# Moving loads and token products between units of a fused RWKV-6 and SiLU-MLP kernel

## The chip, the core and the metric

The kernel runs on one core of a Trainium2 chip. The metric is device time in microseconds, from the start of the program to its end, as a median of several runs. Besides TensorE (PE, with its weight loads PEld), the core has VectorE (DVE), ScalarE (ACT) and GpSimd (POOL); SyncE (SP) issues nearly all DMAs of this kernel, one behind the other.

## The reference

Inputs r, k, v, w have the shape (4 batches, 8 heads, 768 steps, 48). The first part is a recurrence over time, for every batch and head:

```python
state = zeros(48, 48)
for t in range(768):
    y[t] = r[t] @ (state + outer(u * k[t], v[t]))
    state = w[t][:, None] * state + outer(k[t], v[t])
```

The second part takes y as x, 3072 tokens of 384 numbers: `h = x @ w_in` (384 to 2048), `g = h * sigmoid(h)`, `out = g @ w_out` (2048 to 384). Everything is float32.

## The kernel before, in words

**Units.** Time is cut into six blocks of 128 steps and the batches into two pairs: 12 units of 256 tokens (two batches), numbered 0 to 11. Within a unit the recurrence is rewritten as a triangular matrix of scores. Level l of 0 to 6 holds the pairs of steps that lie in neighbouring blocks of 2^l steps; queries (`tr`), keys (`tk`) and products of decays (`tw`) grow from level to level. The diagonal, and in later units all of the small blocks, are not made by matmuls but by products and sums of r, k, u and w in token order: the bonus (`NTOK` is 2, `NPAIR` 4, `NSLOT` 2, `FIRST` 3).

- `level` and `burst` (L698, L706) are the score matmuls, with `keep_level` and `keep_masked` (L716) copying them through a mask into `score`. `prepare` (L774, L621 in `grow_queries`) makes the queries of the next levels on VectorE, and `grow_keys` (L639, L648) the keys on GpSimd.
- Units 0 to 3 form their diagonal with `bonus` (GpSimd, L442 to L446) and `bonus_sum` (VectorE, L451 and L455), which in units 2 and 3 ends with four DMAs into `diag` (L461); `bonus_spread` (L589 to L592) and `bonus_write` (L598) put it into the scores. From unit 4 on `block_bonus` (L501), `block_sum` (L535), `block_move` (L554 to `kept` in memory, L557 back), `block_spread` (L562 to L565) and `block_write` (L571) do this for blocks of eight steps. `load_rk` brings what these need in token order (L107 in units up to 3, L153 later).
- `load_blocks` (L123) brings w, r and k of a unit for the transposes of `turn` (L374), 16 DMAs for each of the three; `raw` has two slots, so a unit's loads may begin when the unit two before it has been turned.
- `y_state`, `y_values` (L847, L855) and `update` (L882) make y and the new state; `move_x` (L918) carries y over ten DMAs to `xt`, the input of the second part.

**Second part.** `up` (L990, then SiLU on ACT at L999) and `down` (L1012) are its two products. From unit 1 on `quarter` (L1056 and the additions L1065) does the second product by a Strassen-like scheme of seven products of 128x192 tiles per half; its operands are sums of halves of g (`sums`, L1038) and four differences of quarters of w_out (`weight_sums`, L1030), each made once.

**Weights.** In the first 100 us the weights of the second part are fetched in 16 pieces (L206) and rounded piece by piece: ACT (L223, L231), VectorE (L242, L243 in `join_weight`) and GpSimd (L255 in `add_weight`).

**Order.** Everything is issued in an order written out by hand: for units 0 to 2 as long `do(...)` lists, after that by `mix(i)`, which returns groups of steps of unit i, with which ups of unit i − 1 and quarters of unit i − 2 are interleaved. Each engine runs its own instructions in that order. Loads of `raw` for coming units are spread over the groups by

```python
loads = block_loads(i + NSLOT) if i + NSLOT < len(units) else []
```

so in `mix(i)` the w, k and r of unit i + 2 are asked for.

Of the kernel before, what the change touches and what calls it, by code (L numbers as in the profile page):

```python
# [8 lines left out]
F32 = mybir.dt.float32  # L9
# [29 lines left out]
def kernel(  # L39
# [11 lines left out]
    nc = tc.nc  # L51

    B, H, S, D = r.shape
    DM, DF = moe_w_in.shape
    L = 128
    NL = 7
    NB = 2
    NP = H // 2
# [7 lines left out]
    units = [(n, b0) for n in range(S // L) for b0 in range(0, B, NB)]  # L66
    NSLOT = 2
    NTOK = 2
    NPAIR = 4
    FIRST = 3  # L70
# [5 lines left out]
    pt = ctx.enter_context(tc.tile_pool(name="pt", bufs=2))  # L76
# [102 lines left out]
    tokens_rk = const.tile([128, 2, H, 2, D], F32, name="tokens_rk")  # L179
# [4 lines left out]
    spare = const.tile([128, NSPARE * 2 * TU], F32, name="spare")  # L184

    def rk(i, x):
        if i < NTOK:
            return twos(raw[:, i % NSLOT, 1 + x])[0].rearrange("p h (s d) -> p h s d", s=2)
        return tokens_rk[:, x]
# [143 lines left out]
    NSC = 1  # L333
    score = const.tile([128, NSC, 2, Q, L], F32, name="score")

    masks = {}
    first = {}
    for l in range(NL):
        c, ni = 1 << l, L >> (l + 1)
# [89 lines left out]
    ruk = {}  # L429
# [4 lines left out]
    def bonus(i, x):  # L434


        engine = nc.gpsimd if i > 0 or x == 0 else nc.vector
        if x == 0:
            ruk[i] = tokens_rk[:, 1] if i < NTOK else pt.tile([128, H, 2, D], F32, name="ruk", bufs=1)

            ruk[i, 0] = tokens_rk[:, 0, :, 0] if i < NTOK else ruk[i][:, :, 0]
            engine.tensor_tensor(out=ruk[i, 0], in0=rk(i, 0)[:, :, 1], in1=rk(i, 1)[:, :, 0], op=ALU.mult)  # L442
        elif x == 1:
            engine.tensor_tensor(out=ruk[i], in0=rk(i, 0), in1=rk(i, 1), op=ALU.mult)
        else:
            engine.tensor_tensor(out=ruk[i], in0=ruk[i], in1=u_bc[:, :, None, :].to_broadcast([128, H, 2, D]), op=ALU.mult)  # L446
# [18 lines left out]
    at = 768  # L465
# [207 lines left out]
    def dims_of(have, start, *dims):  # L673
        return bass.AP(tensor=have.tensor, offset=have.offset + start, ap=[have.ap[0], *dims])

    def corner(l, x):

        return x % 2, x if x % 2 == 0 else (L >> l) - 1 - x
# [2 lines left out]

    def score_products(i, l, queries, sc):
        c, ni = 1 << l, L >> (l + 1)
        if i > 0 or l == NL - 1:
            for p in range(NP):
                for x in range(4 if c == 32 else 2):
                    for e in range(2):
                        rows = slice(PD * e, PD * e + D)
                        if c >= 32:
                            b, first = corner(l, x)  # L690
                            q = (p, 2 * NP - 1 - p)[b]
                            to, have = sc[e][x * c:(x + 1) * c, q, first // 2 * c:(first // 2 + 1) * c], queries[rows, q, (first + 1) * c:(first + 2) * c]
                        else:
                            apart = 2 * (NP - p) - 1
                            to = dims_of(sc[e][x * 64:(x + 1) * 64, p, :], 32 * x, [apart * L // 2 + 32 - 64 * x, 2], [1, 32])
                            have = dims_of(queries[rows, p, :], 64 * x + c, [apart * L + 64 - 128 * x, 2], [2 * c, 32 // c], [1, c])
                        m = 32 if c == 32 else 64
                        nc.tensor.matmul(to, lhsT=tk[i][rows, X[l % 2] + p, x * m:(x + 1) * m], rhs=have, start=True, stop=True)  # L698
            return

        for p in range(NP):
            for e in range(2):
                rows = slice(PD * e, PD * e + D)

                apart, r_p, s_p = 2 * (NP - p) - 1, queries[rows, p, :], sc[e][:, p, :]
                nc.tensor.matmul(bass.AP(tensor=s_p.tensor, offset=s_p.offset,  # L706
                                         ap=[s_p.ap[0], [apart * L // 2, 2], [1, L // 2]]),
                                 lhsT=tk[i][rows, X[l % 2] + p, :],
                                 rhs=bass.AP(tensor=r_p.tensor, offset=r_p.offset + c,
                                             ap=[r_p.ap[0], [apart * L, 2], [2 * c, ni], [1, c]]),  # L710
                                 start=True, stop=True)
# [66 lines left out]
    made = {}  # L778
# [8 lines left out]
    def keep_level(i, l):  # L787
        c = 1 << l
        for e in range(2):
            if c < 32 and (i > NTOK or l == FIRST):  # L790
                keep_masked(i, l, e, made[i, l])
                continue
            for x in range(4 if c == 32 else 2):
                if c >= 32:
                    b, first = corner(l, x)
                    nc.scalar.copy(
                        out=score[x * c:(x + 1) * c, i % NSC, e, b * NP:(b + 1) * NP, (first + 1) * c:(first + 2) * c],
                        in_=made[i, l][e][x * c:(x + 1) * c, b * NP:(b + 1) * NP, first // 2 * c:(first // 2 + 1) * c])
                    continue
                rows = slice(x * 64, (x + 1) * 64)  # L800
                for b in range(NB):
                    half, inner = (x, 1 - x)[b], [1, c]
                    nc.vector.copy_predicated(
                        out=dims_of(score[rows, i % NSC, e, b * NP, :], 64 * half + c, [L, NP], [2 * c, 32 // c], inner),
                        mask=dims_of(masks[l][rows, b], 32 * half, [0, NP], [c, 32 // c], inner),
                        data=dims_of(made[i, l][e][rows, b * NP, :], 32 * half, [L // 2, NP], [c, 32 // c], inner))

    def go_on(i, l):

# [112 lines left out]
    def both(fn, i, *args):  # L922
        return [(fn, i, b, *args) for b in range(NB)]

    def block_loads(i):
        return [(load_blocks, i, name, g) for name in "wkr" for g in range(4)]

    def mix(i):

        ahead = i + 1 < len(units)  # L930
# [37 lines left out]
                      [(block_spread, i), (block_write, i)],  # L968
                      [(burst, i, 5), (keep_level, i, 5), (keep_level, i, 6), (go_on, i, 6)], *end]

        loads = block_loads(i + NSLOT) if i + NSLOT < len(units) else []
        if i + 1 < len(units):
            loads.insert(len(loads) // 2, (load_values, i + 1))

        behind = groups[10 if i < NPAIR else 1:]
        for at, group in enumerate(behind):
            group += loads[at * len(loads) // len(behind):(at + 1) * len(loads) // len(behind)]
        return groups
# [61 lines left out]
    ob, partial = {}, {}  # L1040
# [42 lines left out]
    def do(*steps):  # L1083
        for fn, *args in steps:
            fn(*args)
# [16 lines left out]
    blocks = block_loads(2)  # L1102
# [3 lines left out]
    for l in range(1, NL):  # L1106
# [8 lines left out]
       (up, 0, 2))  # L1115


    others = {1: blocks[8:12], 2: [(bonus_sum, 1, 0), (bonus_sum, 1, 1), (load_rk, 2), *both(update, 0)],
              3: [(bonus_spread, 1), (reverse_v, 1), (clear, 1), (load_values, 2)]}

    def piece(i):
# [3 lines left out]
    for m in range(1, 4):  # L1125
# [1 line left out]
    do((head_weight, 8), (join_weight, 7), (scores, 1, 5), (grow_keys, 1, 6), (add_weight,), (tail_weight, 8), (up, 0, 6),  # L1127
       (bonus_write, 1))

    do((scores, 1, NL - 1), (join_weight, 8), (add_weight,), (up, 0, 7), *both(y, 1), (turn_apart, 1),  # L1130
       (tail_weight, 9), (turn_k, 1), (dense_x, 1, 0), (head_weight, 9, [0]), (dense_x, 1, 1), (head_weight, 9, [1]),
       (join_weight, 9), (add_weight,), (tail_weight, 10), (head_weight, 10), *both(update, 1), (up, 1, 0), *both(turn, 2, "w"))
    blocks = block_loads(3)

    others = {0: [(up, 1, 1), (down, 0, 0, 0), *both(turn, 2, "k"), (product, 2, 0), (product, 2, 1)],
# [4 lines left out]
    for m in range(6):  # L1140
# [2 lines left out]
    second.append(ctx.enter_context(tc.tile_pool(name="po", bufs=1, space=bass.MemoryType.PSUM)))  # L1143

    blocks = block_loads(4)
    do(*blocks[0:2], (level, 2, 2), (prepare, 2, 3), (weight_sums, 1), (down, 0, 1, 0), (down, 0, 0, 3), (down, 0, 1, 1),
       (sums, 1, 0), (bonus, 2, 0), (bonus_sum, 2, 0))
    do(blocks[2], (burst, 2, 3), (keep_level, 2, 3), (keep_level, 2, 4), (go_on, 2, 4), (prepare, 2, 5), (bonus, 2, 1),
       (bonus, 2, 2), (down, 0, 1, 2), (bonus_sum, 2, 1), (load_rk, 3), (sums, 1, 1), *blocks[3:7], (down, 0, 1, 3))
    do((burst, 2, 5), (keep_level, 2, 5), (keep_level, 2, 6), (go_on, 2, 6), (up, 1, 6), (bonus_spread, 2), (bonus_write, 2),  # L1150
       (load_values, 3), (turn_apart, 2), (turn_k, 2), (up, 1, 7), (sums, 1, 2))
    do((sums, 1, 3), (y_state, 2), *both(y_values, 2), *both(update, 2),
       (move_x, 2),
       *blocks[7:])
# [1 line left out]
    for i in range(3, len(units)):  # L1156
        steps = downs(i - 2) + ups(i - 1)
        groups = mix(i)
        if i == NTOK + 1:

            groups[2].append((weight_sums, 2))
            groups[4].insert(1, (weight_sums, 3))
        room = (1, 1, 0, 2, 1, 1, 1, 1, 1, 2, 2, 1, 1, 0) if i < NPAIR else (3, 2, 2, 1, 1, 1, 2, 1, 1, 1, 0)
        for group, count in zip(groups, room):
            do(*group)
            for step in steps[:count]:
                do(*step)
            steps = steps[count:]
# [32 lines left out]
```

## Time and profile before

| what | before |
| --- | --- |
| median of 3 runs | 612.0 us (609.66 to 613.12) |
| profiled execution, its time | 611.3 us |
| its span | 609.5 us |
| mean granted TensorE clock | 0.997 of full speed |
| TensorE busy | 594.1 us, 97% |
| TensorE weight loads | 530.7 us, 87% |
| VectorE | 423.8 us, 70% |
| GpSimd | 367.2 us, 60% |
| ScalarE | 232.7 us, 38% |

All durations are from one profiled execution. A group's line of the timeline gives its start, how long it ran, the engine, the line of the kernel, the operation, output and inputs, the size, and in brackets the idle time of that engine before it with the instruction that ended it. Each float32 matmul of the program stands as two in the counts (L990: 576 calls, x1152). A line of SyncE is the issue of a DMA, not its transfer.

### The profile page before, as it was taken

What the parts mean: (1) busy time and instruction counts of PE and PEld (TensorE: products, weight loads), DVE (VectorE), ACT (ScalarE), POOL (GpSimd) and SP (SyncE); (2) the same over time, 40 slices, a digit from 0 to 9 for tenths busy, and PEclk for the clock granted to TensorE, in tenths of its full rate; (3) what the DMA queues carried; (4) which work ended last, traced back from release to release, by engine and by line L of the source; (5) the groups of instructions that cost most, each with busy time, mean ns of one, the idle gap of its engine ahead of it and who ended that gap; (6) DMA issues with size and microseconds to landing.
All of it is one profiled execution on the core that took longest, in us unless ns stands there. A gap on an engine that the chain in (4) does not pass through costs nothing.

```text
span 609.5 us, 15190 instructions
## 1 busy us (share of the span) xinstructions
PE 594.1 (97%) x5998; PEld 530.7 (87%) x5998; DVE 423.8 (70%) x715; ACT 232.7 (38%) x516; POOL 367.2 (60%) x414
## 2 busy tenths in 40 slices
PE   8999999899999997999999999999999999999997
PEld 7778876699889897889889889989989989989997
DVE  7879779898795495587588587487587597561041
ACT  6799792431530440351351252242252242241110
POOL 6998488557667278378468578568568658500000
PEclk9999999999999998999999999999999999999999
DMA  9966774353543643643543552552452312100000
GB/s 222 300 164 169 147 232 49 72 98 48 128 62 53 135 61 53 129 65 52 121 70 53 113 80 51 108 89 50 97 95 48 81 44 53 36 3 27 26 1 26
DMA packets 203079, 53.44 MB, mean 88 GB/s; under 512 B 186752, under 2 KB 194816, under 8 KB 203008
## 3 DMA queue, kind: packets, MB, share of 16 engines
q1 hardware_dynamic: 201424, 51.88, 41.6%
q8 instruction: 47, 0.77, 0.6%
q10 hardware_dynamic: 1584, 0.59, 0.4%
q14 instruction: 24, 0.20, 0.1%
HBM read 43.21 MB, written 5.24 MB: 79 GB/s over the span
## 4 chain that ended last, share of the span: by engine, by line
PE 72%; DVE 12%; DMA 4%; POOL 3%; ACT 3%; issue 3%; SPq 3%; DVEq 0%; POOLq 0%; ACTq 0%
PE p_h L990 31%; PE p_o L1056 30%; PE p_m L855 2%; DVE score L716 2%; DVE temps L1038 2%; DVE tr L621 2%; SPq L123 2%; PE p_sc L698 2%; POOL tk L639 2%; PE p_m L698 1%; DMA raw<-in_w_dram 1%; PE p_m L847 1%; DMA tokens_w<-in_w_dram 1%; DVE p_w L242 1%; DMA raw<-in_r_dram 1%
## 5 line engine op out<-in xcount | busy, mean ns | idle before, releaser
L990 PE MATMUL p_h<-xt,w_in_sb 128*128 128x256 f32 x1152 | 258.9, 382 | 1.8 <-POOL w_in_sb L255 1.1
L990 PEld LDWEIGHTS p_h<-xt,w_in_sb 128*128 128x128 f32 x1152 | 215.9, 190 | 32.8 <-POOL w_in_sb L255 1.2
L999 ACT ACTIVATE gt<-p_h 128x512 f32<-128x512 f32 x90 | 53.3, 596 | 189.2 <-PE p_h L990 188.8
L639 POOL TENSOR_TENSOR tk<-tk,tw 128x256 f32<-128x256 f32 x128 | 93.7, 753 | 43.5 <-issue 22.9
L1056 PE MATMUL p_o<-own,temps 128*128 128x192 f32 x528 | 90.2, 331 | 4.5 <-DVE temps L1065 4.5
L1056 PEld LDWEIGHTS p_o<-own,temps 128*128 128x128 f32 x528 | 87.6, 193 | 5.4 <-DVE temps L1065 5.3
L1056 PE MATMUL p_o<-w_out_sb,gt 128*128 128x192 f32 x508 | 87.4, 328 | 0.0
L1056 PEld LDWEIGHTS p_o<-w_out_sb,gt 128*128 128x128 f32 x508 | 82.7, 190 | 0.9 <-issue 0.4
L501 POOL TENSOR_TENSOR ruk<-tokens_rk 128x768 f32<-128x768 f32 (+1 forms) x32 | 50.0, 1573 | 52.0 <-DMA tokens_rk<-in_k_dram 31.9
L1038 DVE TENSOR_TENSOR temps<-gt 128x256 f32<-128x256 f32 x84 | 56.9, 677 | 22.4 <-ACT gt L999 22.4
L621 DVE TENSOR_TENSOR tr<-tr,tw 128x512 f32<-128x512 f32 x61 | 56.4, 924 | 15.3 <-PE p_m L698 12.4
L422 POOL TENSOR_TENSOR tw<-tw 128x256 f32<-128x256 f32 (+6 forms) x83 | 43.3, 521 | 36.4 <-DVE tw L374 32.5
L609 ACT COPY tk<-tk 128x256 f32<-128x256 f32 x52 | 20.9, 403 | 99.0 <-POOL tk L639 71.7
L1065 DVE TENSOR_TENSOR partial<-p_o,partial 128x192 f32<-128x192 f32 x33 | 11.8, 358 | 38.9 <-PE p_o L1056 38.7
L1038 DVE TENSOR_TENSOR temps<-temps,gt 128x256 f32<-128x256 f32 x43 | 32.1, 748 | 1.5
L716 DVE COPY_PREDICATED score<-mask,p_sc 128x512 f32<-128x512 int8 x42 | 31.1, 795 | 2.7 <-PE p_sc L698 2.5
L1056 PE MATMUL p_o<-w_out_sb,temps 128*128 128x192 f32 x176 | 30.4, 326 | 0.0
L1065 DVE TENSOR_TENSOR temps<-p_o,partial 128x192 f32<-128x192 f32 x22 | 7.9, 357 | 31.9 <-PE p_o L1056 22.4
L860 ACT COPY yt<-p_m 48x512 f32<-48x512 f32 x40 | 23.2, 581 | 14.9 <-PE p_m L855 8.7
L1056 PEld LDWEIGHTS p_o<-w_out_sb,temps 128*128 128x128 f32 x176 | 28.9, 190 | 0.0
L698 PEld LDWEIGHTS p_sc<-tr,tk 48*32 48x32 f32 (+1 forms) x1312 | 18.1, 119 | 11.6 <-issue 6.3
L501 POOL TENSOR_TENSOR spare<-tokens_rk 128x384 f32<-128x384 f32 (+1 forms) x16 | 28.1, 1754 | 0.0
(180 smaller groups left out, 845.7 us busy)
## 6 DMA issues: line engine op xcount, KB each, us to landing
w_out_sb<-in_moe_w_in_dram SPq DMA_DIRECT2D x6, 768.0 KB, 7.5
w_out_sb<-in_moe_w_out_dram SPq DMA_DIRECT2D x4, 768.0 KB, 5.2
own<-in_moe_w_out_dram SPq DMA_DIRECT2D x4, 768.0 KB, 5.9
tokens_rk<-in_r_dram SPq DMA_DIRECT2D x8, 384.0 KB, 4.4
tokens_rk<-in_k_dram SPq DMA_DIRECT2D x8, 384.0 KB, 5.3
tokens_w<-in_w_dram SPq DMA_DIRECT2D x8, 384.0 KB, 6.5
xt<-yt SPq DMA_DIRECT2D x60, 48.0 KB, 2.0
raw<-in_w_dram SPq DMA_DIRECT2D x80, 32.0 KB, 2.4
```

Source lines behind the costliest of these rows:

```text
L422: engine.tensor_tensor(out=up, in0=t[:, :, 0::2], in1=t[:, :, 1::2], op=ALU.mult)
L501: mul = lambda out, one, two: nc.gpsimd.tensor_tensor(out=out, in0=one, in1=two, op=ALU.mult)
L609: nc.scalar.copy(out=keys(i, X[(l + 1) % 2] * L + c, [4 * c, blocks], [c, 2], [1, c]), in_=keys(i, NP * L + c, [4 * c, blocks], [NP * L + ...
L621: nc.vector.tensor_tensor(out=odd, in0=odd, in1=tw[i][l][:, :, 0::2][:, :, :, None].to_broadcast([128, Q, L >> (l + 1), c]), op=ALU.mult)
L639: nc.gpsimd.tensor_tensor(out=out, in0=have, in1=odd_products(i, l, b, *blocks), op=ALU.mult)
L698: nc.tensor.matmul(to, lhsT=tk[i][rows, X[l % 2] + p, x * m:(x + 1) * m], rhs=have, start=True, stop=True)
L716: nc.vector.copy_predicated(out=dst, mask=masks[l][:, :, None].to_broadcast([128, NB, NP, ni, c]), data=sc[e].rearrange("p (b q) (i c) -> ...
L860: nc.scalar.copy(out=yt[i][PD * e:PD * e + D, :, b, :], in_=p_yt[i, e][PD * b:PD * b + D])
L990: nc.tensor.matmul(p_h[:, a, :], lhsT=w_in_sb[:, c, f * 128:(f + 1) * 128], rhs=xt[i][:, c, :], start=(c == 0), stop=(c == KC - 1))
L999: nc.scalar.activation(out=gt[i, m], in_=p_h, func=AF.Silu)
L1038: nc.vector.tensor_tensor(out=out, in0=one, in1=two, op=op)
L1056: nc.tensor.matmul(p, lhsT=left(f), rhs=right[:, f, :], start=(f == 0), stop=(f == FH - 1))
```

## The change

Four things are moved, and no operation on data is added.

1. The level-4 score products of unit 2 take the form that unit 0 has: 128 columns at once in place of two halves of 64, and so their copy is the whole-bank `keep_masked` in place of eight small ones.
2. The bonus of unit 2 goes from the burst of that unit to the end of unit 1's work and so between the weight pieces. Its token loads (`load_rk(2)`) and those of unit 3, its four `diag` DMAs and the sums of unit 1's bonus go ahead with it. Since `ruk` then still holds another tile, its products are written to `partial` and `spare`.
3. `weight_sums` 1 and 2 go behind the last burst of unit 2.
4. From `mix(4)` on, r is asked for in the unit before its turn, and no longer two units before: `mix(3)` loads only w and k of unit 5, `mix(4)` loads r of unit 5 with w and k of unit 6 in its groups behind `block_move`, and so on to `mix(10)`, which loads r of unit 11 alone. The number of DMAs is the same.

```diff
@@ bonus
         if x == 0:
-            ruk[i] = tokens_rk[:, 1] if i < NTOK else pt.tile([128, H, 2, D], F32, name="ruk", bufs=1)
+            if i == NTOK:
+                free = pt.tile([128, 4, DM // 2], F32, name="partial", bufs=1)
+                ruk[i] = free.rearrange("p x d -> p (x d)").rearrange("p (h s d) -> p h s d", h=H, s=2)
+            else:
+                ruk[i] = tokens_rk[:, 1] if i < NTOK else pt.tile([128, H, 2, D], F32, name="ruk", bufs=1)
...
+            if i == NTOK:
+                ruk[i, 0] = spare[:, 0:H * D].rearrange("p (h d) -> p h d", h=H)
@@ score_products
-        if i > 0 or l == NL - 1:
+        if (i > 0 or l == NL - 1) and (i, l) != (NTOK, FIRST + 1):
@@ keep_level
-            if c < 32 and (i > NTOK or l == FIRST):
+            if c < 32:
                 keep_masked(i, l, e, made[i, l])
                 continue
...
-                rows = slice(x * 64, (x + 1) * 64)
-                for b in range(NB):
-                    half, inner = (x, 1 - x)[b], [1, c]
-                    nc.vector.copy_predicated(
...
@@ mix
-        loads = block_loads(i + NSLOT) if i + NSLOT < len(units) else []
+        loads = [*at(i >= NPAIR and ahead, *block_loads(i + 1, "r")), *at(i + NSLOT < len(units), *block_loads(i + NSLOT, "wk"))]
         if i + 1 < len(units):
             loads.insert(len(loads) // 2, (load_values, i + 1))
 
-        behind = groups[10 if i < NPAIR else 1:]
+        behind = groups[10 if i < NPAIR else 4 if i == NPAIR else 1:][:4 if i + NSLOT >= len(units) else None]
@@ the lists of units 1 and 2
-    others = {1: blocks[8:12], 2: [(bonus_sum, 1, 0), (bonus_sum, 1, 1), (load_rk, 2), *both(update, 0)],
+    others = {1: [(bonus_sum, 1, 0), (bonus_sum, 1, 1), (load_rk, 2), *blocks[8:12]], 2: [*both(update, 0)],
...
-    do((scores, 1, NL - 1), (join_weight, 8), (add_weight,), (up, 0, 7), *both(y, 1), (turn_apart, 1),
+    do((scores, 1, NL - 1), (bonus, 2, 0), (bonus, 2, 1), (join_weight, 8), (add_weight,), (bonus_sum, 2, 0), (bonus, 2, 2), (up, 0, 7), *both(y, 1), (turn_apart, 1),
...
-       (join_weight, 9), (add_weight,), (tail_weight, 10), (head_weight, 10), *both(update, 1), (up, 1, 0), *both(turn, 2, "w"))
+       (join_weight, 9), (add_weight,), (tail_weight, 10), (head_weight, 10), *both(update, 1), (bonus_sum, 2, 1), (load_rk, 3), (up, 1, 0), *both(turn, 2, "w"))
...
-    do(*blocks[0:2], (level, 2, 2), (prepare, 2, 3), (weight_sums, 1), (down, 0, 1, 0), (down, 0, 0, 3), (down, 0, 1, 1),
-       (sums, 1, 0), (bonus, 2, 0), (bonus_sum, 2, 0))
-    do(blocks[2], (burst, 2, 3), (keep_level, 2, 3), (keep_level, 2, 4), (go_on, 2, 4), (prepare, 2, 5), (bonus, 2, 1),
-       (bonus, 2, 2), (down, 0, 1, 2), (bonus_sum, 2, 1), (load_rk, 3), (sums, 1, 1), *blocks[3:7], (down, 0, 1, 3))
-    do((burst, 2, 5), (keep_level, 2, 5), (keep_level, 2, 6), (go_on, 2, 6), (up, 1, 6), (bonus_spread, 2), (bonus_write, 2),
-       (load_values, 3), (turn_apart, 2), (turn_k, 2), (up, 1, 7), (sums, 1, 2))
+    do(*blocks[0:2], (level, 2, 2), (prepare, 2, 3), (down, 0, 1, 0), (down, 0, 0, 3), (down, 0, 1, 1), (sums, 1, 0))
+    do(blocks[2], (burst, 2, 3), (keep_level, 2, 3), (keep_level, 2, 4), (go_on, 2, 4), (prepare, 2, 5), (down, 0, 1, 2),
+       (bonus_spread, 2), (sums, 1, 1), *blocks[3:7], (down, 0, 1, 3))
+    do((burst, 2, 5), (keep_level, 2, 5), (keep_level, 2, 6), (go_on, 2, 6), (bonus_write, 2), (up, 1, 6), (weight_sums, 1),
+       (load_values, 3), (turn_apart, 2), (turn_k, 2), (up, 1, 7), (weight_sums, 2), (sums, 1, 2))
@@ the loop over units 3 to 11
-            groups[2].append((weight_sums, 2))
             groups[4].insert(1, (weight_sums, 3))
```

## The prediction

> **What bounds the kernel now.** I read the busy table and the 40 slices first, then TensorE's timeline with its idle times, then the timelines of VectorE and SyncE around the two largest of them.
>
> ```profile
> PE 594.1 (97%) x5998; PEld 530.7 (87%) x5998; DVE 423.8 (70%) x715; ACT 232.7 (38%) x516; POOL 367.2 (60%) x414
> ...
> PEclk9999999999999998999999999999999999999999
> ```
>
> TensorE is busy 97% of 609.5 us, so what the change can win is TensorE's own waits, and work that it takes off TensorE; faster side engines alone win nothing. The one low digit of the clock is slice 16 (229 to 244 us). TensorE's timeline from 110 to 250 us (start, duration, idle time before and who ended it in brackets):
>
> ```profile
> 113.82 0.75 PE L698 MATMUL p_sc<-tr,tk 48*32 48x32 f32 x64 [1.56 <-DVE tr L621]
> 114.84 0.69 PE L698 MATMUL p_o<-tr,tk 48*64 48x64 f32 x32 [0.27 <-DVE tr L774]
> ...
> 137.54 0.69 PE L698 MATMUL p_m<-tr,tk 48*64 48x64 f32 x32 [0.95 <-POOL tk L639]
> ...
> 183.41 5.47 PE L1056 MATMUL p_o<-own,temps 128*128 128x192 f32 x32 [1.22 <-DVE temps L1065]
> ...
> 233.43 7.15 PE L1056 MATMUL p_o<-own,temps 128*128 128x192 f32 x32 [3.33 <-DVE temps L1065]
> ```
>
> These five are 7.33 us. Before 100 us the timeline has smaller ones, about 3.4 us together (0.74 at 35, 0.57 at 45 and 1.05 at 62.78 are the largest); after 246 us none is above 0.05. The same 32 matmuls take 5.47 us at 183 and 7.15 us at 233: 1.68 us more, because the clock is halved there for about 3.4 us.
>
> VectorE ahead of the first gap:
>
> ```profile
> 102.00 2.22 DVE L1030 TENSOR_TENSOR own<-w_out_sb,own 128x1536 f32<-128x1536 f32 x1
> ...
> 107.63 0.54 DVE L451 TENSOR_REDUCE own_sums<-ruk 128x8 f32<-128x384 f32 x1
> ...
> 109.29 2.03 DVE L803 COPY_PREDICATED score<-mask,p_o 64x128 f32<-64x128 int8 x8
> 111.35 2.32 DVE L621 TENSOR_TENSOR tr<-tr,tw 128x512 f32<-128x512 f32 x1
> ```
>
> VectorE runs without rest from 97 to 118 us, and TensorE waits for the last line, the queries of level 5. For the 3.33 us gap, SyncE's queue:
>
> ```profile
> 188.81 9.12 SPq L123 DMA_DIRECT2D raw<-in_r_dram  x16
> 198.03 3.85 SPq L123 DMA_DIRECT2D raw<-in_w_dram  x8
> ...
> 203.28 0.33 SPq L554 DMA_DIRECT2D kept<-block_sums  x1
> ```
>
> and VectorE in the same stretch:
>
> ```profile
> 209.13 0.01 DVE L565 LOAD_MASK_SELECT spare<-spare  x1 [8.03 <-ACT spare L564]
> ```
>
> The sums of unit 4's blocks are ready at 197.76 us, but their transfer `kept` is issued at 203.28, behind 16 loads of r of unit 5 and 8 of w. VectorE idles 8.03 us for it and resumes 11.4 us after the sums. One unit later the sums are ready at 249.47, `kept` is issued at once (249.49), VectorE resumes at 256.66 (7.2 us) and TensorE has no gap. In the late unit the tokens also land late (215.58), so GpSimd's products L501 (212.38 to 218.69) run beside VectorE's sums L1038: 1.92, 2.03, 1.21 and 1.23 us against 0.42 alone. The unit's transposes start 22.3 us after the sums instead of 18.4; L1065, which must read and free TensorE's accumulator, comes 3.3 us too late.
>
> **What the Trainium skill says.** "TensorE: Matmul & The Clock Gate", section "What's actually happening": after an idle window of about 3.4 us the array falls to half clock. The trace agrees: the 3.33 us gap cost the clock, the gaps of 1.56 and 1.22 didn't. "SBUF — State Buffer", section "Who interferes with whom": a VectorE instruction with two SBUF inputs contends with a GpSimd one that reads SBUF. It agrees: L1038 at 0.42 and 2.03, L621 at 0.68 and 2.32 us. "TensorE: Matmul & The Clock Gate", section "The mechanism" of Part 3: small matmuls at different places of the array overlap. It agrees: 32 of the 48x64 kind take 0.69 us.
>
> **The change part by part**, against the profiled execution (span 609.5, its time 611.3; the median of the runs is 612.0, so a span of S is read as S + 2.5).
>
> *Level 4 of unit 2.* Its 32 matmuls 48x64 (0.69 us with drain, about 0.47 of issue) become 16 of 48x128, the form of L706; sixteen of those stand in the trace as 1.18 us, about 0.90 of issue. On TensorE: **+0.43 us**. On VectorE the eight small copies L803 (2.03) become two whole-bank L716 copies (1.29): −0.74.
>
> *Bonus of unit 2.* On GpSimd 1.18 + 1.81 + 1.80 us leave 105 to 113 us for 64 to 72 us, where the trace has GpSimd idle 3.5, 4.4 and 2.3 us between weight rounds. On VectorE 0.54 leaves the path of L621, and the 1.00 behind it. With no L446 beside it L621 falls from 2.32 to about 0.9 (its neighbours: 0.68, 1.11). The sums of unit 1 run a piece earlier: 1.5 us on VectorE, which may delay the weight round of 53.60 by some 0.8 to 1.3; the gap of 1.05 at 62.78, a wait for GpSimd, takes that up. If that cover is gone it costs up to 0.5. The products now lie in `partial` and in `spare`; their last reader, the sum, runs before unit 1's first up, so before `spare` is written by an activation and long before unit 1's quarters use `partial`: no wait (`spare` is first written again by unit 1's fourth up).
>
> *Weight differences 1 and 2* (2.22 at 102.00 and 2.21 at 133.53) go behind unit 2's diagonal copy L598 (122 us). Their first readers are matmuls of unit 1's quarters at 130.59 and later, and VectorE idles 2.26 us at 118 to 120 for ACT's `both_b`, so most of their 4.4 us is covered. Without that cover they would stand before the `state` work at 124 us and cost up to 2. ACT's copies of `both_b` now precede the L796 copies; ACT is busy 38%, so this is nothing, and L592 comes earlier by the L796 copies' length.
>
> *Sum for the early gaps.* VectorE's path to L621 loses 2.22 + 0.54 + 0.74 + 1.4 = 4.9 us against 1.83 needed: **−1.83**. The gap of 0.95 at 137: VectorE loses the 2.21 in front of unit 3's transposes, and L639, which runs at 1.66 and 1.18 us beside L1030, falls toward 0.65: **−0.95**.
>
> *DMAs.* Eight issues (four `diag`, four tokens of unit 3, 5.3 us) move from 115.7–121.2 to before the last two loads of `own` weights (issued 77.62 and 81.30, SyncE idle about 4.8 us there). These loads may be issued some 1 to 4.7 us later. ACT's L223 reads the first at 87.19, it lands at 83.57 now: late by 0 to 1.5 us, which the matmul L1012 at 100.49 sees. I take 0.3. The trace doesn't show the two in this order: bounds 0 and 1.5.
>
> *r one unit later.* From mix(3) 16 loads vanish (7.9 us of queue) before `kept` of unit 4; in mix(4) the r of unit 5 goes behind tokens and `block_move`. `kept` then is issued on time, as in the next unit: 11.4 becomes about 7.2 us, the tokens land some 5.5 us earlier, L1038 mostly runs at 0.42. 4 us are won on VectorE against 3.33: **−3.33**, and the clock **−1.68**. What is late next: r of unit 5, issued from +4.5 to +16 us after the sums, landing by about +18, wanted by the third pair of transposes at about +20.8: 2.8 us of margin. `move_x` of unit 4 follows; its xt lands about 4 us ahead of the first up. In mix(5) to mix(10) the count ahead of `kept` stays 8 (r in place of w), so it is on time there too; r lands about 7 us ahead.
>
> *Unchanged:* the gap of 1.22 at 182. Its chain (burst, copies, tokens of unit 4 beside L1038) moves with TensorE as a whole. Bounds: −1.22 to +1.5.
>
> Sum: −1.83 − 0.95 − 3.33 − 1.68 + 0.43 + 0.3 = −7.1. Span 602.4, time **604.9 us**.
>
> **Rivals.**
> (A) *The stall moves.* With `kept` on time the next one in line, r of unit 5 or xt or L1065 itself, is late by half of the gap: the margins after the stalled unit are small (in the next one L1065 ends at 281.22, and TensorE's quarter before the one that needs it ends at about 281.7: 0.5 us). Then 3 to 5 us of the 5.0 stay, the early gaps are won: −7.1 + 4 = −3, **609 us**. For it: that margin; against: the same steps close without a gap in every later unit.
> (B) *Nothing measurable.* VectorE's moved 4.4 us or the later weight loads cost elsewhere what the early gaps gave (the 1.22 gap grows, L1012 waits 1.5) and the stall stays: −0.5 to −1, **611.5 us**.
> (C) *Slower: r is late in every unit.* It is asked for one unit nearer to its turn in seven units. If it lands more than about 0.5 us after its transposes each late microsecond goes to TensorE seven times. It decides from 7.1/7 + 0.5 = 1.5 us late per unit; at 2.5 us late, 7 × 2.0 − 7.1 = +7, **619 us**. Against: r's last loads are issued about 11 us after the sums, its transposes come 20 us after them, and loads in this queue land some 2.4 us after issue (8 deep behind a token load, up to 7).
> (D) *More:* the 1.22 gap goes too: **603.7 us**.
>
> **How the numbers follow.** Forecast, with D: 0.64; A 0.17; B 0.10; C 0.09. Half a per cent is 3.06 us, about what a measurement of this kernel can tell from no change: faster is below 608.9, slower above 615.1. A splits (0.10 faster, 0.07 same); C splits (0.07 slower, 0.02 same); B splits (0.07 same, 0.03 slower). Faster 0.74, same 0.16, slower 0.10. The forecast's own range is 603 to 607.5: bounds of the weight loads (+1.2), of the 1.22 gap (−1.2, +1.5), and the runs' own spread. Holding A and part of B: **602 to 611**.
>
> **What would show it.** Right: TensorE's gaps at about 112, 135 and 228 us gone, no 0.5 clock after the last, L1056 back at 5.47 us; `kept` issued within 0.5 us of the last L535 in unit 4; VectorE's idle time before its L565 about 4 instead of 8 us. A: a smaller gap in the same place, ended by L1065 or a transfer of `raw`. C: transposes L374 released by `raw<-in_r_dram` in several units. Also wrong if L1012 or the ups around 100 us show a wait for L255 above 1.5 us, or if VectorE's moved L1030 delay unit 1's quarters at 128 us.

## The result, and the profile after

| | before | after |
| --- | --- | --- |
| median | 611.9 us (609.66 to 613.22, 6 runs) | 605.9 us (604.98 to 607.39, 6 runs) |
| ratio | | 0.9908, 95% interval 0.9884 to 0.9932 |
| profiled execution, its time and span | 611.3, 609.5 us | 607.4, 605.6 us |
| TensorE busy | 594.1 us (97%) | 593.4 us (98%) |
| TensorE's gaps above 0.15 us from 30 us on | 9.7 us | 6.1 us |
| mean granted clock | 0.997 | 1.000 |

The forecast was 604.9 (602 to 611). The profiled execution after happens to be the longest of its six: the others' spans are 603.2 to 605.5. By the ratio, which compares runs of one session, the change wins 5.6 us (4.2 to 7.1).

TensorE's timeline of the changed kernel, from 20 to 300 us (start, duration, engine, line, operation, shapes; in brackets the idle time before it and who ended it):

```profile
89.34 0.70 PE L704 MATMUL p_sc<-tr,tk 48*64 48x64 f32 x32 [0.55 <-POOL tk L669]
...
107.14 1.16 PE L712 MATMUL p_o<-tr,tk 48*128 48x128 f32 x16
108.23 5.43 PE L1009 MATMUL p_m<-w_out_sb,gt 128*128 128x384 f32 x16
113.59 0.76 PE L704 MATMUL p_sc<-tr,tk 48*32 48x32 f32 x64
114.28 0.69 PE L704 MATMUL p_o<-tr,tk 48*64 48x64 f32 x32
...
136.12 0.69 PE L704 MATMUL p_m<-tr,tk 48*64 48x64 f32 x32
...
183.33 5.47 PE L1053 MATMUL p_o<-own,temps 128*128 128x192 f32 x32 [2.38 <-DVE temps L1062]
...
227.20 7.96 PE L1053 MATMUL p_o<-own,temps 128*128 128x192 f32 x48
...
277.71 5.47 PE L1053 MATMUL p_o<-own,temps 128*128 128x192 f32 x32 [1.39 <-DVE temps L1062]
```

The gaps of 1.56, 0.27, 0.95 and 3.33 us have no bracket any more. At 227.20 the quarter before the old stall and the one behind it run as one group: 48 matmuls in 7.96 us at full clock. In their place the wait near 182 us has grown from 1.22 to 2.38, and one of 1.39 us stands a unit later, near 276. (The lines are numbered six higher or three lower than before: 1053 is the old 1056, 1062 the old 1065, 1035 the old 1038, 704 the old 698, 712 the old 706.)

SyncE's queue after, at the sums of unit 4 and of unit 5:

```profile
197.71 0.33 SPq L560 DMA_DIRECT2D kept<-block_sums  x1
199.30 1.00 SPq L563 DMA_DIRECT2D spare<-kept  x2
...
202.32 10.96 SPq L123 DMA_DIRECT2D raw<-in_r_dram  x16
...
240.43 3.90 SPq L123 DMA_DIRECT2D raw<-in_r_dram  x8
...
245.40 0.64 SPq L560 DMA_DIRECT2D kept<-block_sums  x1
248.99 1.00 SPq L563 DMA_DIRECT2D spare<-kept  x2
```

In unit 4 `kept` goes out at 197.71, as its sums end (197.68), with the loads of r behind it. In unit 5 the sums are ready at 244.04 (the end of L541), but eight loads of r of unit 6 and two outputs are ahead, and `kept` goes out 1.4 us late. It is then slow to land as well: SyncE can fetch it back (L563) 3.6 us after its issue, against 1.6 in unit 4. VectorE's waits for the two:

```profile
204.89 0.01 DVE L571 LOAD_MASK_SELECT spare<-spare  x1 [3.85 <-ACT spare L570]
...
252.87 0.01 DVE L571 LOAD_MASK_SELECT spare<-spare  x1 [5.47 <-ACT spare L570]
```

Before, unit 4 had 8.03 here and unit 5 had 3.86. The lateness has moved on by one unit and is much smaller.

### The profile page after: what moved, and what is told of

The parts are those of the page before. It is cut to its first block, busy times and chain, and to the rows that moved or that the text cites. A ratio compares the mean times of both kernels' runs of the same rounds, so it can differ in the third digit from the quotient of the medians.

```text
span 605.6 us, 15147 instructions
## 1 busy us (share of the span) xinstructions
PE 593.4 (98%) x5982; PEld 529.5 (87%) x5982; DVE 416.8 (69%) x709; ACT 233.2 (39%) x516; POOL 366.6 (61%) x414
## 4 chain that ended last, share of the span: by engine, by line
PE 75%; DVE 8%; DMA 5%; POOL 3%; ACT 3%; SPq 2%; issue 2%; DVEq 0%; POOLq 0%; ACTq 0%
PE p_h L987 31%; PE p_o L1053 31%; PE p_m L1009 3%; PE p_m L852 2%; PE p_sc L704 2%; DMA tokens_w<-in_w_dram 2%; POOL tk L645 2%; DVE temps L1035 2%; PE p_m L704 1%; SPq L123 1%; PE p_m L844 1%; DVE score L722 1%; DVE tr L627 1%; DMA u_bc<-in_u_dram 1%; DVE p_w L242 1%
## 5 line engine op out<-in xcount | busy, mean ns | idle before, releaser
L645 POOL TENSOR_TENSOR tk<-tk,tw 128x256 f32<-128x256 f32 x128 | 91.2, 734 | 42.8 <-issue 22.9
L1053 PE MATMUL p_o<-own,temps 128*128 128x192 f32 x528 | 88.7, 327 | 3.8 <-DVE temps L1062 3.8
L1053 PEld LDWEIGHTS p_o<-own,temps 128*128 128x128 f32 x528 | 86.0, 190 | 4.7 <-DVE temps L1062 4.6
L507 POOL TENSOR_TENSOR ruk<-tokens_rk 128x768 f32<-128x768 f32 (+1 forms) x32 | 51.3, 1613 | 49.6 <-DMA tokens_rk<-in_k_dram 25.5
L1035 DVE TENSOR_TENSOR temps<-gt 128x256 f32<-128x256 f32 x84 | 55.8, 664 | 22.4 <-ACT gt L996 22.4
L1062 DVE TENSOR_TENSOR partial<-p_o,partial 128x192 f32<-128x192 f32 x33 | 11.8, 358 | 38.3 <-PE p_o L1053 38.1
L1035 DVE TENSOR_TENSOR temps<-temps,gt 128x256 f32<-128x256 f32 x43 | 32.2, 748 | 1.5
L1062 DVE TENSOR_TENSOR temps<-p_o,partial 128x192 f32<-128x192 f32 x22 | 7.9, 357 | 32.7 <-PE p_o L1053 23.3
L507 POOL TENSOR_TENSOR spare<-tokens_rk 128x384 f32<-128x384 f32 (+1 forms) x16 | 29.3, 1833 | 0.0
```

The source lines that it names most:

```text
L507: mul = lambda out, one, two: nc.gpsimd.tensor_tensor(out=out, in0=one, in1=two, op=ALU.mult)
L645: nc.gpsimd.tensor_tensor(out=out, in0=have, in1=odd_products(i, l, b, *blocks), op=ALU.mult)
L1035: nc.vector.tensor_tensor(out=out, in0=one, in1=two, op=op)
L1053: nc.tensor.matmul(p, lhsT=left(f), rhs=right[:, f, :], start=(f == 0), stop=(f == FH - 1))
```

## The experiments

All ratios are to the kernel before, run on the same chip in the same session (medians 611.9 us beside the changed kernel, 611.65 beside e1 to e4, 611.5 beside e5 to e8); one kernel has 4 to 15 runs. Across sessions the ratios compare, not the medians. The gaps are those of one profiled execution each.

| run | median us | ratio, 95% interval | gap near 182 | gaps after 190 us |
| --- | --- | --- | --- | --- |
| before | 611.5 to 611.9 | | 1.22 | 3.33 and 1.68 of clock |
| after | 605.9 | 0.9908 (0.9884 to 0.9932) | 2.38 | 1.39 |
| e1, only r | 608.4 | 0.9948 (0.9934 to 0.9961) | 1.70 | 0.23 |
| e2, only the early parts | 608.3 | 0.9950 (0.9934 to 0.9966) | 1.27 | 2.28 and the clock |
| e3, tokens of unit 4 ahead | 607.1 | 0.9935 (0.9912 to 0.9959) | none | 1.36 |
| e4, r of unit 6 behind too | 606.1 | 0.9921 (0.9898 to 0.9944) | 0.94 | 1.33 |
| e5, after once more | 606.4 | 0.9911 (0.9890 to 0.9932) | 2.43 | none |
| e6, r behind everywhere | 605.0 | 0.9892 (0.9869 to 0.9916) | 1.61 | none |
| e7, e6 and tokens of unit 4 | 604.5 | 0.9883 (0.9862 to 0.9904) | 1.21 | none |
| e8, e7 with level 4 as before | 604.0 | 0.9874 (0.9850 to 0.9899) | 1.11 | none |

**Which part won what?** In the first profile after, TensorE reached the quarter behind the 182 gap at 183.33 us against 183.41 before: all that the early parts had won seemed lost there. That was theory 1. Its rival was the prediction's own sum.

The r part alone, in the kernel before:

```diff
-    def block_loads(i):
-        return [(load_blocks, i, name, g) for name in "wkr" for g in range(4)]
+    def block_loads(i, names="wkr"):
+        return [(load_blocks, i, name, g) for name in names for g in range(4)]
...
-        loads = block_loads(i + NSLOT) if i + NSLOT < len(units) else []
+        loads = [*at(i >= NPAIR and ahead, *block_loads(i + 1, "r")), *at(i + NSLOT < len(units), *block_loads(i + NSLOT, "wk"))]
...
-        behind = groups[10 if i < NPAIR else 1:]
+        behind = groups[10 if i < NPAIR else 4 if i == NPAIR else 1:][:4 if i + NSLOT >= len(units) else None]
```

> The kernel before with the moved loads of r alone; the early parts stay as before. Theory 1 (the early parts' gain is swallowed by the wait near 182 us, whose end is set by when the tokens of unit 4 can be asked for in SyncE's queue): the early gaps of 1.56, 0.27 and 0.95 us stay, the gap near 182 stays at about 1.2, the 3.33 near 230 and its halved clock are gone, a gap of about 1.4 stands near 276 as in the changed kernel; span about 605.5 and time within 0.5 us of the changed kernel. Rival (the parts add up, as in the prediction): the r part alone gives only 3.33 + 1.68 less what comes back at 276, and the early parts another 2.3 on top, so this kernel is 2 us or more slower than the changed one.

The early parts alone: the same diff, reversed, in the changed kernel.

> The changed kernel with the loads of r where they were before (two units ahead); the early parts stay. Theory 1: no gap at 112 and 136, but the gap near 182 is 2.4 us instead of 1.2, the gap near 230 is there with 3 us or more and the halved clock, and the time is that of the kernel before within 0.5 us (about 611.9). Rival (the parts add up): about 2.3 us faster than before, 609.5.

By the ratios each part gives about half: −3.2 us (interval −4.0 to −2.4) and −3.1 (−4.0 to −2.1), against −5.6 for both. Theory 1 fell on both counts: e1 was not within 0.5 us of the changed kernel, nor e2 of the kernel before. In e1's profile the stall near 230 and its halved clock are gone, as both theories had it, but the early gaps did not stay as they were: 1.14 at 90, 0.89 at 115, 0.36 at 122 and 1.20 at 139, though the edit changes nothing in SyncE's order before 169 us. Waits there differ between executions. TensorE's timeline of e2 around the two gaps:

```profile
181.80 5.47 PE L1053 MATMUL p_o<-own,temps 128*128 128x192 f32 x32 [1.27 <-DVE temps L1062]
...
230.71 7.15 PE L1053 MATMUL p_o<-own,temps 128*128 128x192 f32 x32 [2.28 <-DVE temps L1062]
```

The quarter at 181.80 is 1.6 us ahead of before with the gap unchanged (1.22, 1.27): the chain does move with TensorE, as the prediction had it. And the stall of unit 4 is a third smaller though r was not moved, because `kept` goes out at 200.62 against 203.28, 2.7 us sooner while TensorE is 1.6 sooner. Its length fell by the difference, 1.05 us. Part of one stall is thus won by either part, and is counted twice if the two are added. The ratios would put it at 3.2 + 3.1 − 5.6 = 0.7 us, which is less than their intervals; the trace of e2 is what shows it.

**Is the wait near 182 set by the tokens?** The tokens of unit 4 are asked for ahead of the `diag` transfers, and eight loads of r of that unit go behind:

```diff
-                      [(burst, i, 3), (keep_level, i, 3), (bonus_sum, i, 0), (bonus, i, 1), (bonus, i, 2)],
-                      [(keep_level, i, 4), (go_on, i, 4), (bonus_sum, i, 1), (load_rk, i + 1), (load_u,)],
+                      [(burst, i, 3), (keep_level, i, 3), (bonus_sum, i, 0), (bonus, i, 1), (bonus, i, 2), (load_rk, i + 1)],
+                      [(keep_level, i, 4), (go_on, i, 4), (bonus_sum, i, 1), (load_u,), *block_loads(i + 1)[10:12]],
...
-       *blocks[7:])
+       *blocks[7:10])
```

> The changed kernel, with the tokens of unit 4 asked for before the diag transfers of unit 3 and before the last eight loads of r of unit 4, which go behind them. Theory 1: tokens issued near 149.5 instead of 155.0 us, GpSimd's products near 156 to 162 and so out of the way of VectorE's sums, transposes near 166.5 instead of 169.9, the 2.38 gap gone. What is won there is then partly taken back near 276, where the tokens of unit 5 stand in the same queue: that gap grows from 1.39 to 1.4 to 3.8; time 0 to 2.4 us below the changed kernel. Rival (the wait near 182 is VectorE's own chain behind unit 3's burst, and moves with TensorE): the gap stays at 2 us or more although the tokens come sooner.

The gap at 182 is gone. By itself that does not show that the tokens set it, for TensorE now comes there later, held by two new waits. What shows more is VectorE: its eight sums L1035 take 3.0 us (165.38 to 168.41) where the first profile of the changed kernel has 7.0 (163.03 to 170.00), and L1062, which ends the wait, comes 1.6 us sooner although the sums begin 2.4 us later. The first and the last of the eight in the changed kernel:

```profile
163.03 1.25 DVE L1035 TENSOR_TENSOR temps<-gt 128x256 f32<-128x256 f32 x1 [2.76 <-ACT gt L996]
...
169.58 0.42 DVE L1035 TENSOR_TENSOR temps<-gt,temps 128x256 f32<-128x256 f32 x1
```

The time is not better (607.1). TensorE and VectorE of e3:

```profile
158.14 5.45 PE L987 MATMUL p_h<-xt,w_in_sb 128*128 128x256 f32 x24 [1.00 <-ACT gt L996]
165.41 2.86 PE L987 MATMUL p_h<-xt,w_in_sb 128*128 128x256 f32 x12 [1.82 <-ACT gt L996]
```

```profile
157.84 4.23 DVE L604 COPY_PREDICATED score<-own_mask,both_b 128x1024 f32<-128x1024 int8 x2
161.97 1.49 DVE L627 TENSOR_TENSOR tr<-tr,tw 128x512 f32<-128x512 f32 x1
...
165.38 0.43 DVE L1035 TENSOR_TENSOR temps<-gt 128x256 f32<-128x256 f32 x1 [1.92 <-ACT gt L996]
...
167.99 0.42 DVE L1035 TENSOR_TENSOR temps<-gt,temps 128x256 f32<-128x256 f32 x1
```

GpSimd's products L507 now run from 154.89 to 162.9 beside the diagonal copy L604, which takes 4.23 us instead of 2.51, and the sums L1035 are free of them (0.43). ACT's copies L801 wait for L604, its SiLU stands behind them, and TensorE waits 1.00 and 1.82 us for that. The collision was moved, not removed.

**What is late next, near 276?** r of unit 6 goes behind the tokens as well:

```diff
-        behind = groups[10 if i < NPAIR else 4 if i == NPAIR else 1:][:4 if i + NSLOT >= len(units) else None]
+        behind = groups[10 if i < NPAIR else 4 if i <= NPAIR + 1 else 1:][:4 if i + NSLOT >= len(units) else None]
```

> The changed kernel, with the loads of r of unit 6 also put behind the transfer of unit 5's sums and its tokens, as the change does one unit earlier. Theory 1: that transfer is issued at about 244.0 instead of 245.4, the tokens some 3 to 5 us sooner, VectorE's sums beside GpSimd's products are shorter, the 1.39 gap near 276 is gone; time 1.4 us below the changed kernel (about 604.5); the gap of 2.38 near 182 is unchanged. Rival (the gap near 276 is VectorE's own chain, or r of unit 6 then comes too late): the gap stays or another of 1 us or more stands in its place.

The 276 gap is gone, and one of the same size stands one unit on, where `kept` goes out 2.7 us after the sums, behind the eight loads of r of unit 7:

```profile
322.81 5.47 PE L1053 MATMUL p_o<-own,temps 128*128 128x192 f32 x32 [1.33 <-DVE temps L1062]
```

The time is no better than the changed kernel's, where 1.4 less was expected. The next two runs separate what is drawn by chance from what stands in the queue.

> The changed kernel once more, beside the three kernels below. It tells what is fixed in the gaps near 182 and 276 us and what is drawn anew by each execution. Theory 2 (the tokens of unit 4 take 6.6 us to land in the first profile of the changed kernel and 5.0 to 5.6 in the four others, and the gap follows the landing): the gap near 182 is about 1.2 with a landing near 5.2 us, and the span of the profiled execution is 1 us or more below 605.6. Theory 1 (the early gain is swallowed there): the gap is 2.4 again. Time about 606.

The same program, profiled once more, has no gap at 276, but 2.43 at 182 and one of 0.67 at 158. So the 1.39 is not fixed. Four profiles have the eight loads of r of unit 6 ahead of `kept`; in each it goes out late, and what differs most is how long it then takes until SyncE can fetch it back:

| unit 5 | `kept` issued after its sums | fetched back after that | gap near 276 |
| --- | --- | --- | --- |
| after | 1.36 us | 3.59 us | 1.39 us |
| e3 | 1.54 | 3.35 | 1.36 |
| e1 | 1.82 | 1.69 | 0.23 |
| e5 | 0.86 | 2.12 | none |
| e4, loads behind | 0.03 | 1.55 | none |

Of e1, the two lines are:

```profile
248.56 0.40 SPq L554 DMA_DIRECT2D kept<-block_sums  x1
250.25 1.00 SPq L557 DMA_DIRECT2D spare<-kept  x2
```

The gap follows the sum of the two and not the lateness in the queue alone: e1 is the latest there and has almost no gap. A sum of 3.0 us (e5) costs nothing. No run varied the landing by itself, and why one transfer takes 1.7 and another 3.6 us behind the same loads is open.

The 182 gap follows how far GpSimd's products reach into VectorE's sums. In the changed kernel's two profiles they start 7.2 us after the tokens are asked for and 0.8 us ahead of the first sum (162.19 and 163.03; 163.37 and 164.16), with gaps of 2.4. In e4 and e6, whose order is the same up to there, they start 5.8 and 6.0 us after the request and 2.3 and 2.0 us ahead, with gaps of 0.94 and 1.61 (in e6 the second product waits another 0.64 for u). Counted from the first sum to the end of the products, the nine profiles with the tokens behind `diag` run from 3.8 us (e4, gap 0.94) over 4.4 (before, 1.22) and 4.9 (e1, 1.70) to 5.3 (e5, 2.43). Theory 2 held in that the gap follows the landing; it failed in expecting a quick landing here. Why the products start 1.2 us later in two executions of the changed kernel and in none of the eight others (5.75 to 6.2 us after the request) is open.

Then r behind the tokens in all units:

```diff
-        behind = groups[10 if i < NPAIR else 4 if i == NPAIR else 1:][:4 if i + NSLOT >= len(units) else None]
+        behind = groups[10 if i < NPAIR else 4:][:4 if i + NSLOT >= len(units) else None]
```

> The changed kernel, with r put behind the unit's tokens in every unit from 4 on, and not in unit 4 alone. In the run with r of unit 6 moved the gap of 276 was gone, and one of 1.33 stood at 321, behind the eight loads of r of unit 7. Theory (what is left after the r part is SyncE's queue, which falls behind TensorE by the eight loads ahead of the unit's sums, one unit after another): no gap from 230 us to the end, time about 1 us below the changed kernel, 605. Rival (the gap only moves on to other units, or r comes late at its transposes): gaps of 1 us or more after 230, same time or longer.

No gap above 0.05 us is left between 183 and the end. SyncE's queue of this run at unit 5:

```profile
236.46 4.03 SPq L123 DMA_DIRECT2D raw<-in_k_dram  x8
240.59 0.40 SPq L1066 DMA_DIRECT2D out_dram<-ob  x1
241.08 0.38 SPq L1066 DMA_DIRECT2D out_dram<-temps  x1
243.09 0.33 SPq L560 DMA_DIRECT2D kept<-block_sums  x1
```

The queue rests before `kept`, which goes out as the sums end (243.06). The time is 1.4 us below the repeat of the changed kernel on the same chip, as expected in size, but the intervals of the two overlap, and the two profiles do not put it down to this edit: e5 has no gap after 190 us either, and the two differ in the waits at 158 (0.67 and none) and 182 (2.43 and 1.61), ahead of anything that the edit moves.

**Two versions beyond the change.** With the tokens behind `diag` where they were, and eight loads of r of unit 4 behind the tokens, on top of e6:

```diff
-                      [(keep_level, i, 4), (go_on, i, 4), (bonus_sum, i, 1), (load_rk, i + 1), (load_u,)],
+                      [(keep_level, i, 4), (go_on, i, 4), (bonus_sum, i, 1), (load_rk, i + 1), (load_u,), *block_loads(i + 1)[10:12]],
...
-       *blocks[7:])
+       *blocks[7:10])
```

> As the kernel with r behind the tokens everywhere, and the last eight loads of r of unit 4 put behind that unit's tokens, which stay behind the diag transfers of unit 3 (ahead of them the products collided with the copy into the diagonal, 4.23 against 2.51 us, and TensorE waited 1.00 and 1.82 for it). Tokens asked for near 153.5 instead of 155.0 and landing in 4.5 to 5 us for 5 to 6.6; VectorE's sums collide for half as long; the gap near 182 falls below 0.5, no new one at 157 or 164. Time 1 to 2 us below the kernel with r behind the tokens everywhere, about 604. Rival: the tokens wait for something else than the queue and the gap stays near 1.2.

The tokens go out at 153.97 and the products start 6.0 us later, no sooner than in e6: the landing is not what the r loads cost, only 0.8 us of queue is. The gap is 1.21, not below 0.5. The time, 604.5, is 0.5 us below e6's where 1 to 2 were expected, and the intervals overlap: no gain of this edit is shown.

Last, level 4 of unit 2 in its old form, on top of e7:

```diff
-        if (i > 0 or l == NL - 1) and (i, l) != (NTOK, FIRST + 1):
+        if i > 0 or l == NL - 1:
...
-            if c < 32:
+            if c < 32 and (i > NTOK or l == FIRST):
                 keep_masked(i, l, e, made[i, l])
                 continue
...
```

> As the kernel before this one in the list, with level 4 of unit 2 in its old form: 32 half-width matmuls in the count of the profile, and eight small copies. The prediction priced the new form at +0.43 us on TensorE; the trace of the changed kernel has 0.62 (from 106.52 to 108.23 against 105.74 to 106.83). Theory: TensorE is behind no wait between 90 and 180 us, the old copies cost VectorE 0.74 that it can spare, so this kernel is 0.4 to 0.6 us faster. Rival: the old copies bring back a wait at 112 us of 0.5 or more, same time or longer.

TensorE's timeline of this run (its line 1018 is the down, 1009 above):

```profile
106.94 0.69 PE L704 MATMUL p_sc<-tr,tk 48*64 48x64 f32 x32
107.46 0.65 PE L704 MATMUL p_o<-tr,tk 48*64 48x64 f32 x32
108.03 5.43 PE L1018 MATMUL p_m<-w_out_sb,gt 128*128 128x384 f32 x16
113.39 0.76 PE L704 MATMUL p_sc<-tr,tk 48*32 48x32 f32 x64
```

From the first burst to the down behind it is 1.09 us, against 1.71 in the changed kernel: the new form costs 0.62 us, and the old copies bring no wait back at 113. The medians differ by 0.5 us, of the expected sign and size, which the intervals can't tell apart; the trace does. This is the fastest version run: 7.5 us (ratio 0.9874) below the kernel before.

## Why the prediction was right

Step by step, on TensorE's timeline, measured from its first up (35.99 before, 36.20 after), which takes out what the start differs by.

- *The early sum.* At unit 3's second burst the changed kernel is ahead by (137.54 − 35.99) − (136.12 − 36.20) = 1.63 us; the prediction's early terms are −1.83 − 0.95 + 0.43 + 0.3 = −2.05. All three gaps are closed, and with the two costs as measured below (0.62 and 0.55) the sum is −1.61. VectorE's L621 of unit 2 fell to a mean of 0.87 us for three, from 1.37.
- *Level 4* was priced at +0.43 and cost 0.62. The step that failed took the issue of 16 wide matmuls as 0.90 us; the trace before has 1.09 to 1.11 for this form (L706 from 13.12 to 14.23 and from 20.82 to 21.91, where the next instruction starts). Here they take 107.14 to 108.23, 1.09 us, and the first burst before them no longer overlaps their start (0.62 to the next against 0.52). Both forms stream as many columns (16 times 128, 32 times 64); that the narrow one needs about half the time fits the overlap of small matmuls that the prediction counted on, which its 0.69 us does not show by itself.
- *The weight loads* were given 0.3 at L1012, for a piece up to 1.5 us late. ACT does wait 1.70 us for that piece (L223 at 89.16), but no matmul of L1009 waits. The wait came elsewhere: 0.55 at 88.79, ended by GpSimd's key product, behind another piece of w_out that now lands in ACT's way (ACT waits 0.82 us for it at 80.91). In the other runs with the new order it is 0.26 to 0.42, but e1, with the old one, has 1.14 there and the kernel before nothing: part of it is drawn anew by each execution. The sums of unit 1, run a piece earlier, cost 0.49 at 54 us and were covered by the 1.05 gap at 62.78, now 0.12, as said.
- *The stall of unit 4* was priced at −3.33 and −1.68, and is gone in all eight profiles with the r part. But e1 gives −3.2 us in all, not −5.0. The term that was mis-sized is the 3.33. In 29 runs of the kernel before the mean granted clock is 0.997 or less in 24, 0.994 in eight of these, and 0.999 or 1.0 in five; one halving of 3.4 us is 0.003 of the span. In e1 it is 0.997 in four of 15, in e2 in five of 14, in the changed kernel in none of 12. The means (0.9966 before, 0.9991 in e1) make the clock's share of e1's gain about 1.5 us (an estimate: their difference times the span), near the 1.68, and leave about 1.7 for the stall, where the intervals are 0.8 wide to either side. In the two profiles the price does hold: from the quarter behind the 182 gap to the end are 426.1 us before and 421.2 in e1. But the price was taken from the one profile that the kernel before has; what the stall costs in its other runs is open. The clock, too, was booked on r alone, and e2, in which the stall is only shortened, wins part of it. Why the r part alone loses the clock in a quarter of its runs was not tried.
- *"In mix(5) to mix(10) the count ahead of `kept` stays 8, so it is on time there too"* was wrong for mix(5): `kept` is 0.9 to 1.8 us late there in all four profiles with the eight loads ahead. The count did stay, but TensorE is 5.4 us further on there (240.29 against 245.71 at unit 5's first burst), and SyncE, which issues without rest from 202 to 246, is not. That is rival A in small: a gap of 1.39 us, in one of the changed kernel's two profiles. In all four with the eight loads behind (e4, e6, e7, e8) `kept` goes out as the sums end and the gap is gone.
- *The gap at 182, "moves with TensorE as a whole"*, holds in e2 (1.27), and its upper bound of +1.5 was used nearly in full in both profiles of the changed kernel (2.38, 2.43: +1.2).
- *Rival C*, r late in every unit, did not happen, not even with all 16 loads behind the tokens in every unit (e6): no transpose waits for it.

The median came out 1.0 us above the forecast of 604.9; by the ratio 5.6 of the 7.1 us summed were won. By parts: the r part alone gave 1.8 less than priced (3.2 for 5.0), the early parts 1.0 more (3.1 for 2.05), and 0.7 is won by either and counts once. So the mechanism held, the waits named are gone, and that the total fell so near is in part luck: errors of 1.8 and 1.0 us have opposite signs.

## What to carry to other kernels

When a wait is closed ahead of a serial DMA queue, the consumer moves forward and the queue does not, so the next unit's margin has to be worked out from the queue's own issue times, and from the landing behind bulk loads, not from a count of DMAs that stays. Put the short transfer that a chain waits for ahead of bulk loads in every repetition of a loop, not only where the profile shows the stall now (e6 has no gap left behind 183 us; that it is faster is within the noise). A loss seen in one profiled execution (a halved clock, a slow landing) can differ in the next: give it the share of runs in which it happens.

## What the runs showed of the hardware

The clock fell after a gap well short of the 3.4 us idle window that the prediction cited from the Trainium skill ("TensorE: Matmul & The Clock Gate", section "What's actually happening"). Engine busy time and granted clock of e2 by stretches of 1 us (columns: stretch, length, then busy us of PE, PEld, DVE, ACT and POOL with instructions, granted clock, DMA share, GB/s):

```profile
229.00:230.00 1.00, 0.00 (x0) 0.00 (x0) 1.00 (x2) 0.00 (x0) 0.11 (x1) 1.00 0.29 77
230.00:231.00 1.00, 0.29 (x2) 0.29 (x3) 0.97 (x4) 0.00 (x0) 1.00 (x2) 1.00 0.15 39
231.00:232.00 1.00, 1.00 (x6) 1.00 (x6) 0.52 (x1) 0.00 (x0) 1.00 (x1) 0.63 0.27 76
232.00:233.00 1.00, 1.00 (x5) 1.00 (x4) 0.59 (x3) 0.00 (x0) 0.93 (x2) 0.50 0.19 48
```

TensorE was idle for 2.28 us (228.43 to 230.71), and the clock halved about 0.5 us after it had resumed (the 0.63 of its stretch puts the fall at 231.26), for some 3.4 us; the 32 matmuls took 7.15 us instead of 5.47, as after the 3.33 gap before. The gaps of 2.38 and 2.43 in the changed kernel's two profiles cost no clock. The same page says that the window runs free of the program, which would make it a matter of where a gap falls; this fits, but no run varied it. Second, a masked copy in which mask and data come from SBUF (L604) is slowed by GpSimd's reads as an addition of two tensors is: 4.23 us beside L507 in e3, 2.51 alone in the changed kernel.
